# Second batch's scores in visits of six banks, a new order of q and k transposes, third batch's order, and the last output block in three pieces

## The chip, the cores and the metric

The kernel runs on one core of one Trainium2 chip. The metric is the device time of one execution in microseconds: the median of three runs before the change is 350.76 us (350.17 to 351.44). The engines are named as in the profile: PE is TensorE (matrix products; PEld its weight loads), DVE VectorE, ACT ScalarE, POOL GpSimd, SP the engine that issues transfers.

## The reference

An attention with beacon keys and values, and a mixer behind it. 8 batches, 8 heads, 576 queries, 16 beacons, head size 64.

```python
k_all = np.concatenate([beacon_k, k], axis=2)
v_all = np.concatenate([beacon_v, v], axis=2)
scores = scale * np.matmul(q, k_all.transpose(0, 1, 3, 2))
scores = np.where(causal, -1000000000.0, scores)
a = np.exp(scores - scores.max(-1, keepdims=True))
a /= a.sum(-1, keepdims=True) + 1e-09
x = np.matmul(a, v_all)              # then [batch, 576, 8 * 64]
...
h = x.transpose(0, 2, 1) @ U @ V     # U [576, 32], V [32, 576]
u = x + h.transpose(0, 2, 1)
out = u + np.maximum(u @ w_ch1, 0.0) @ w_ch2    # 512 -> 2048 -> 512
```

## The kernel before

**Tiling.** The work of attention is counted in pairs of heads: pair `p` is batch `p // 4` and heads `2 * (p % 4)` and the next, so pairs 0 to 3 are the first batch, 4 to 7 the second, 8 to 11 the third. The mixer's two large products run over eight full blocks of 512 rows and a last one (4608 rows are nine blocks). A block has 16 `g_unit`s (line 539: four products of 128x512 each, then a relu on ScalarE or VectorE into `gT`) and four output row blocks of 128, each in four quarters (`c_unit`, line 554: quarter `part` multiplies the slices `4 * part` to `4 * part + 3` of `gT` and `w2`, and the fourth adds u and stores).

**Steps of a pair.** `qkT_of(p)` has two units, which transpose q and k on TensorE into a bank of PSUM and copy them out on VectorE; their source is either the loaded tile itself or, after `regroup_of(p)`, a copy of it by token that VectorE makes. `scores_of(p)` gives units: the first two score groups, the last two, and the masks. There are four groups of keys; a group takes one bank for each head of the pair. A *visit* computes some groups, each into its banks, and ScalarE takes the exponential of each bank into the `expt` tiles. `visit` at line 373 takes any list of (pair, group), also of two pairs. Masks are applied by VectorE behind the exponentials; for pairs 0, 1 and 4 (`ON_PE`) instead by products of TensorE ahead of the scores. `av_of(p)` has a unit for each head: 15 products of probabilities and values into one bank, then VectorE's reciprocal and product into `xb`. The `expt` tiles are four, so pair p and pair p + 2 share them.

**PSUM.** `pst` (line 105) takes the bank that was given back longest ago in the order of the code, so an allocation waits for the user of eight allocations earlier.

**Order.** Every engine's order is that of the code (`manual_schedule`, line 788). The units of the mixer stand in `queue`, and `fill(n)` (line 754) issues the next n of them between steps of attention. When a batch's attention is done, `mix(b)` (line 771) puts the low-rank mixer's steps (`head`, `most`, `end`) and four empty places (`None`) into the queue and calls `feed`, which appends the blocks that have become possible. Block 0 covers the first 512 rows, all of the first batch; its 16 `g_unit`s and 16 quarters are the only units in the queue while the second batch's attention runs.

**Loads.** GpSimd issues the loads of q, k, v and of the weights, all in the order of the code: the first batch, then `emit_w1` quarters between loads of the second batch, then `emit_w2` (line 191) in two halves (slices 0 to 7 and 8 to 15), then the third batch (`load_batch(2)`).

**DMA transposes.** From batch 4 on q and k are transposed by DMA: `turns` (line 650) makes ten transfers, which SP issues (`kTs`, `qTs`; five blocks j each of k and q, in the order k0, q0, k1, q1, ...). SP also issues the transposes of `xb` into `uT`, those of `uT` into `ut`, and the stores.

**Last block.** `c_half` (line 581) computes the very last 128 rows in two halves of 256 columns, each stored by SP when it is done.

Of the kernel before, what the change touches and what calls it, by code (L numbers as in the profile page):

```python
# [18 lines left out]
P = 128  # L19
# [11 lines left out]
def kernel(  # L31
# [486 lines left out]
    def mlp_units(t0, n, dst, flip, turned=True, last=False):  # L518
# [59 lines left out]
                emptying(ps)  # L578
                nc.sync.dma_start(out=dst(i, m), in_=ob[:m, :])

        def c_half(i, part):
            hs = ds(DM // 2 * (part // 2), DM // 2)
            if part % 2 == 0:
                cps["t"] = pst([P, DM // 2], F32, name="cph")
            for dc in range(NDC // 2 * (part % 2), NDC // 2 * (part % 2 + 1)):
                nc.tensor.matmul(  # L586
                    cps["t"], gT["t"][:, dc, ts(i, P)], w2[:, dc, hs], start=(dc == 0), stop=(dc == NDC - 1)
                )
            if part % 2:
                ob = outp.tile([P, DM // 2], F32, name="oh", tag="ob")  # L590
                nc.vector.tensor_tensor(out=ob, in0=cps["t"], in1=gT["u"][:, i, hs], op=ALU.add)
                emptying(cps["t"])
                nc.sync.dma_start(out=dst(i, P)[:, hs], in_=ob)

        units += [lambda dc=dc: g_unit(dc) for dc in range(NDC)]
        for i in range((n + P - 1) // P):
            c = c_half if last and i == n // P - 1 else c_unit
            units += [lambda i=i, part=part, c=c: c(i, part) for part in range(4)]
        return units, g_part

# [49 lines left out]
    def turns(b):  # L650

        new_qT(b)
        kn, qn = Ls[b][1]
        us = []
        for j in range(NT):
            for n, dst, o, m in ((kn, kTs[b % 2], P * j, nk[j]), (qn, qTs[b], q0[j], nq[j])):
                us.append(
                    lambda n=n, dst=dst, o=o, m=m, j=j: nc.sync.dma_start_transpose(
                        out=dst[:, :, ds(o, m)], in_=n[:m, j, :, :].rearrange("p h d -> p (h d)")
                    )  # L660
                )
        return us

    HALVES = [slice(0, H // 2), slice(H // 2, H)]
    SETS = [slice(2 * c, 2 * c + 2) for c in range(NH2)]
# [67 lines left out]


    NF = 2
    ON_PE = (0, 1, 4)
    AHEAD = 16

    DT0 = 4
    LAG = 10  # L740
    HINT = 5

    FIRST = [3, 3, 2, 1]

    IDLE = [8, 1, 1, 0, 1]
    queue = []
# [7 lines left out]
    def fill(n):  # L754
        while n > 0 and queue:
            u = queue.pop(0)
            if u is not None:
                u()
            n -= 1

    def feed(b):

        while state["t"] < NBLK and 512 * (state["t"] + 1) <= S * (b + 1):
            t = state["t"]
            units, state["part"] = mlp_units(
                512 * t, 512, lambda i, m, t=t: rows[ds(512 * t + P * i, m), :], t % 2, t > 0, t == NBLK - 1
            )
            queue.extend(units)
            state["t"] += 1

    def mix(b):

        turned = b >= NF
        turn, head, parts = mix_units(xbs[b], S * b, turned)
        if turned:
            turn()
        n = 0 if not turned else LAG + 3 if b == B - 1 else min(LAG, len(queue) - 8)
        k = 2 if turned else 1
        most, end = parts
# [6 lines left out]
        feed(b)  # L786

    with tc.manual_schedule(engines={ENG.PE, ENG.Activation, ENG.DVE, ENG.SP, ENG.Pool}):
        load_first()
# [77 lines left out]
        begin(2, (3,))  # L867
        part(D2, 2)
        rest(2, 2, (act_copy, V), act_copy)
        t0, sc = qkT_of(4), scores_of(4)  # L870
        t0[1]()
        t0[0]()
        part(D3, 2)
        fill(4)
        fill(1)
        sc[0]()
        for u in qkT_of(5):
            u()
        fill(1)

        sc[1]()
        fill(1)
        sc = scores_of(5)
        sc[0]()

        NP1 = NF * NH2
        for p in range(NH2, NP1):
            b, c = divmod(p, NH2)
            if c == 0:
                load_batch(b + 1)  # L890
            seq = []
            masks = lambda: None
            if p + 2 < NP1:
                seq += [lambda i=i, p=p: qkT_of(p + 2)[i]() for i in range(2)]
            if p + 3 < NP1:
                seq.append(lambda p=p: regroup_of(p + 3))
            if p + 1 < NP1:
                seq.append(sc[1])
                masks = sc[2]
            av = av_of(p)  # L900
            if p + 2 == NP1:
                masks = lambda: None
                av = [lambda u=u, m=sc[3], i=i: (u(), m(i)) for i, u in enumerate(av)]
            seq += av
            sc = []
            if p + 2 < NP1:
                new_qT_of(p + 2)
                sc = scores_of(p + 2)
                seq.append(sc[0])
            seq.append(masks)  # L910
            done = 0
            for i, u in enumerate(seq):
                u()
                want = FIRST[c] * (i + 1) // len(seq)
                fill(want - done)
                done = want
            if c == NH2 - 1:
                mix(b)

        fill(AHEAD - 8)  # L920
        regroup_of(NP1)
        regroup_of(NP1 + 1)
        fill(8)
        t0, t1 = qkT_of(NP1), qkT_of(NP1 + 1)
        for u in t0 + [lambda: visit([(NP1, 0), (NP1, 1)])] + t1:
            u()
            fill(1)
        regroup_of(NP1 + 2)
        visit([(NP1, 2), (NP1, 3), (NP1 + 1, 0)])
        fill(1)  # L930
        tr = []


# [64 lines left out]
                    masks_of(p + 1)  # L998
                    fill(1)

        def slot(p, c, av, qk):

            if c == 0:
                regroup_of(p + 3)
                qk[0]()
                fill(1)
                masks_of(p)
                qk[1]()
                fill(1)
                go([(p + 1, 1), (p + 1, 2), (p + 1, 3)])  # L1010
                fill(1)
                av[0]()
                av[1]()
                fill(1)
            elif c == 1:
                regroup_of(p + 3)
                qk[0]()
                fill(1)
                masks_of(p)
                go([(p + 1, 0), (p + 1, 1), (p + 1, 2)])  # L1020
                fill(1)
                qk[1]()
                av[0]()
                fill(1)
                av[1]()
                fill(1)
            elif c == 2:
                regroup_of(p + 3)
                go([(p, 3), (p + 1, 0), (p + 1, 1)])
                fill(1)  # L1030
                masks_of(p)
                qk[0]()
                fill(1)
                av[0]()
                qk[1]()
                av[1]()
                fill(1)
            else:
                regroup_of(p + 3)
                go([(p, 2), (p, 3), (p + 1, 0)])  # L1040
                fill(1)
                qk[0]()
                fill(1)
                qk[1]()
                fill(1)
                masks_of(p)
                go([(p + 1, 1), (p + 1, 2), (p + 1, 3)])
                fill(1)
                av[0]()
                av[1]()  # L1050
                masks_of(p + 1)
                fill(1)

        for p in range(NP1, NP):
            b, c = divmod(p, NH2)
            if c == (1 if b >= DT0 else 0) and b + 1 < B:
                load_batch(b + 1)
            if c == (1 if b + 1 == DT0 else 2) and DT0 <= b + 2 < B:
                load_whole(b + 2)
            qk = qkT_of(p + 2) if p + 2 < min(NP, DT0 * NH2) else []  # L1060
# [10 lines left out]
            (slot if p < P6 else long_slot)(p, c, av_of(p), qk or [lambda: None] * 2)  # L1071
        mix(B - 1)
        guard()

# [106 lines left out]
```

## Time and profile before

| | |
|---|---|
| median of 3 runs | 350.76 us |
| profiled execution, own time | 351.05 us |
| its span | 349.4 us |
| granted TensorE clock, mean | 0.999 |
| TensorE on the chain that ended last | 94% |
| ScalarE, VectorE on it | 2%, 3% |
| DMA traffic | 41.89 MB, mean 120 GB/s |

The page shows busy time by engine, the span in 40 slices, the DMA queues, the chain of work that ended last, and the costliest groups of instructions. A row of the timeline has the start and the length in microseconds, the engine, the line of the code, the operation, what it writes and reads (`out<-in`), the shape, and how many instructions were merged; in brackets, the idle time of the engine before it and what the profile believes ended it. Matrix products are pipelined and their ends are modelled, so lengths of neighbours overlap; the difference of two starts is the better price. A row `DMA to landing us min/median/max` gives the time from the issue of a transfer to its last byte.

### The profile page before, as it was taken

How to read it: one execution, taken by the hardware profiler on the slowest of the kernel's cores; microseconds unless marked ns; L12 is line 12 of the kernel's file. 1: busy time of each engine (PE TensorE's matmuls, PEld its weight loads, DVE VectorE, ACT ScalarE, POOL GpSimd, SP SyncE). 2: the span in 40 equal slices, each digit the busy share in tenths (PEclk: the TensorE clock that was granted, in tenths of full speed). 3: DMA queues.
4: the chain of work that ended last, by engine and by line, in shares of the span. 5: the costliest groups of instructions: out<-in, count | busy, mean ns of one | idle time of the engine just before them, and what ended most of it. 6: DMA issues, size and time to landing. Idle time of an engine off the chain costs nothing.

```text
span 349.4 us, 7796 instructions
## 1 busy us (share of the span) xinstructions
PE 342.3 (98%) x3084; PEld 173.6 (50%) x3084; DVE 190.4 (55%) x492; ACT 163.7 (47%) x358; POOL 97.9 (28%) x137
## 2 busy tenths in 40 slices
PE   8999999999999999999999999999999999999995
PEld 4565565555554455444554545445444444444443
DVE  5776965788875653654465456535555642323311
ACT  5967851577823665167615753484334203302400
POOL 8886714553505447303740140000000000000000
PEclk9999999999999999999999999999999999999999
DMA  9999999999998999992999798713122314013011
GB/s 165 133 188 175 158 199 176 228 134 146 129 145 134 168 134 124 148 232 16 126 136 157 167 117 125 176 43 68 63 75 47 69 62 120 2 60 105 16 66 65
DMA packets 146636, 41.89 MB, mean 120 GB/s; under 512 B 131488, under 2 KB 142080, under 8 KB 146592
## 3 DMA queue, kind: packets, MB, share of 16 engines
q0 software_dynamic: 87440, 18.18, 69.8%
q1 hardware_dynamic: 58928, 22.84, 36.6%
q8 instruction: 26, 0.43, 0.6%
q10 hardware_dynamic: 224, 0.30, 0.3%
q14 instruction: 18, 0.15, 0.2%
HBM read 37.37 MB, written 9.44 MB: 134 GB/s over the span
## 4 chain that ended last, share of the span: by engine, by line
PE 94%; DVE 3%; ACT 2%; issue 0%
PE gps L534 36%; PE cps L560 35%; PE po L397 8%; PE sps L382 6%; ACT expt L354 2%; PE tps L275 1%; PE sps L348 1%; PE idle L250 1%; PE cph L586 1%; PE qtp L434 1%; PE tps L281 1%; PE ups L459 1%; DVE qT L308 1%; PE ups L413 1%; DVE xb L406 0%; DVE kT L308 0%
## 5 line engine op out<-in xcount | busy, mean ns | idle before, releaser
L534 PE MATMUL gps<-uT,w 128*128 128x512 f16 x576 | 136.2, 379 | 0.4 <-DVE qT L308 0.2
L560 PE MATMUL cps<-w,gT 128*128 128x512 f16 x560 | 130.8, 379 | 0.0
L388 ACT ACTIVATE expt<-sps 128x496 f16<-128x496 f32 x192 | 82.5, 534 | 71.7 <-PE sps L382 71.7
L547 ACT ACTIVATE gT<-gps 128x512 f16<-128x512 f32 x86 | 51.0, 620 | 79.2 <-PE gps L534 79.0
L534 PEld LDWEIGHTS <-w 128*128 128x128 f16 x576 | 51.8, 98 | 57.8 <-issue 2.5
L560 PEld LDWEIGHTS <-gT 128*128 128x128 f16 x560 | 50.8, 98 | 59.2 <-issue 6.2
L549 DVE TENSOR_SCALAR gT<-gps 128x512 f16<-128x512 f32 x58 | 39.9, 690 | 42.3 <-PE gps L534 40.9
L573 DVE TENSOR_TENSOR ob<-cps,ut 128x512 f32<-128x512 f32 x31 | 21.4, 691 | 48.3 <-PE cps L560 47.5
L218 POOL DMA_DIRECT2D vs<-in_v_dram x50 | 39.6, 806 | 17.4 <-PE gps L534 4.5
L397 PEld LDWEIGHTS <-expt 128*128 128x128 f16 (+1 forms) x960 | 36.3, 98 | 12.8 <-issue 1.0
L397 PE MATMUL po<-vs,expt 128*128 128x65 f16 (+1 forms) x960 | 38.9, 194 | 0.1
L406 DVE TENSOR_TENSOR xb<-po,rec 128x320 f16<-128x320 f32 x64 | 31.5, 492 | 2.2
L324 DVE TENSOR_TENSOR expt<-expt,bigmask 128x512 f16<-128x512 f16 x58 | 24.1, 416 | 6.7 <-ACT expt L388 6.7
L354 ACT ACTIVATE expt<-sps 128x496 f16<-128x496 f32 (+1 forms) x64 | 27.0, 606 | 1.0 <-PE sps L348 1.0
L405 DVE RECIPROCAL rec<-po 128x5 f32<-128x5 f32 x64 | 12.1, 188 | 26.9 <-PE po L397 26.7
L382 PE MATMUL sps<-qT,kT 64*128 64x80 f16 (+4 forms) x288 | 23.4, 281 | 0.4 <-DVE gT L549 0.3
L646 POOL DMA_DIRECT2D st<-in_q_dram x20 | 16.8, 856 | 11.3 <-DMA st<-in_k_dram 5.3
L382 PEld LDWEIGHTS <-kT 64*128 64x128 f16 x288 | 9.9, 94 | 18.8 <-issue 15.3
L200 POOL DMA_DIRECT2D vs<-in_beacon_v_dram x8 | 4.3, 536 | 53.5 <-PE po L397 53.5
L646 POOL DMA_DIRECT2D st<-in_k_dram x20 | 16.9, 867 | 4.3 <-DMA st<-in_q_dram 3.3
L446 DVE TENSOR_TENSOR uT<-ups,uT 128x496 f16<-128x496 f32 x24 | 14.5, 668 | 5.0 <-PE ups L459 5.0
L308 DVE COPY qT<-tps 128x576 f16<-128x576 f16 (+1 forms) x16 | 11.8, 735 | 3.9 <-PE tps L281 2.3
(97 smaller groups left out, 164.3 us busy)
## 6 DMA issues: line engine op xcount, KB each, us to landing
out_dram<-ob SPq DMA_DIRECT2D x35, 256.0 KB, 2.5
vs<-in_v_dram POOLq DMA_DIRECT2D x18, 128.0 KB, 7.2
w<-in_moe_w_ch_dram POOLq DMA_DIRECT2D x4, 512.0 KB, 6.8
w<-in_moe_w_ch_dram POOLq DMA_DIRECT2D x2, 1024.0 KB, 14.1
st<-in_k_dram POOLq DMA_DIRECT2D x12, 128.0 KB, 10.9
st<-in_q_dram POOLq DMA_DIRECT2D x12, 128.0 KB, 10.9
st<-in_k_dram POOLq DMA_DIRECT2D x2, 576.0 KB, 13.4
st<-in_q_dram POOLq DMA_DIRECT2D x2, 576.0 KB, 16.2
```

Source lines behind the costliest of these rows:

```text
L218: nc.gpsimd.dma_start(out=dst[a : a + nq[j], j, :, :], in_=src[hs, ds(q0[j], nq[j]), :].rearrange("h p d -> p h d"))
L324: nc.vector.tensor_tensor(out=e4, in0=e4, in1=bigmask, op=ALU.min)
L354: nc.scalar.activation(out=ex[i][:, ds(SLOT * g, gw[g])], in_=ps[g, i][:, 0 : gw[g]], func=AF.Exp, scale=scale)
L382: nc.tensor.matmul(ps[p, g, i][:, ds(o, w)], kT[hp, c, ds(P * ch, P)], qT[hp, c, ds(qa, w)], start=True, stop=True,)
L388: nc.scalar.activation(out=at[p][3][i][:, ds(SLOT * g, gw[g])], in_=ps[p, g, i][:, 0 : gw[g]], func=AF.Exp, scale=scale)
L397: nc.tensor.matmul(po[:, j, :], ex[0 : nk[c], ds(blk[(c, j)], P)], vs[0 : nk[c], ds(c * H * E + h * E, E)], start=(c == 0), stop=(c == j),)
L406: nc.vector.tensor_tensor(out=xb[:, :, ds(h * D, D)], in0=po[:, :, 0:D], in1=r.broadcast_to([P, NT, D]), op=ALU.mult)
L534: nc.tensor.matmul(g[:, 0:n], w1[:, cc, ts(dc, P)], uT[:, cc, ds(t0, n)], start=(cc == 0), stop=(cc == NCC - 1))
L547: nc.scalar.activation(out=gT["t"][:, dc, 0:n], in_=g[:, 0:n], func=AF.Relu)
L549: nc.vector.tensor_scalar_max(out=gT["t"][:, dc, 0:n], in0=g[:, 0:n], scalar1=0.0)
L560: nc.tensor.matmul(ps[:m, :], gT["t"][:, dc, ds(P * i, m)], w2[:, dc, :], start=(dc == 0), stop=turned and dc == NDC - 1, skip_group_check ...
L646: nc.gpsimd.dma_start(out=dst[a : m[j], j, :, :], in_=src[:, ds(q0[j], nq[j]), :].rearrange("h p d -> p h d"))
```

## The change

**Second batch.** The loop over pairs 4 to 7 with its counts (`FIRST`) is replaced by four lines of words, which a new function `play` issues. A word names a step and a pair: `f` one unit of the queue, `q` and `k` the two transposes, `r` the regrouping, `a` and `b` the values of the two heads, `m` (or `n`, `o` for one head) the masks, `e4:01` the groups 0 and 1 of pair 4 with masks by TensorE, and `v5:3,6:01` a visit of group 3 of pair 5 and groups 0 and 1 of pair 6. The old order, in the same words, from the first visit of pair 4 on:

```
f e4:01 q5 k5 f e4:23 f v5:01 q6 k6 r7 f v5:23 a4 b4 f v6:01 m5 f
q7 k7 v6:23 f a5 b5 f v7:01 m6 f
v7:23 a6 n7 f b6 o7 f
a7 b7 f
```

The new order is in the diff. From the first visit of pair 4 until `mix(1)` the queue gives 15 units instead of 11 (with the five ahead of it 20 instead of 16); behind `mix(1)` it gives 4 instead of 8 ahead of `regroup_of(8)`.

**Third batch.** The start of its order is written in words, and its four slots too. Against the old order, q11's transposes stand at the end of the first slot, ahead of the fill and of `regroup_of(12)`, where they stood behind it.

**DMA transposes.** `turns` issues k0, q0, q1, q2, q3, q4, k1, k2, k3, k4.

**Last block.** `c_piece` computes the last 128 rows in pieces of 256, 128 and 128 columns (48 products where there were 32); the last piece is stored by ScalarE.

```diff
-        def c_half(i, part):
-            hs = ds(DM // 2 * (part // 2), DM // 2)
...
+        def c_piece(i, part):
+            o, w, d0, d1 = [
+                (0, 2 * P, 0, NDC // 2), (0, 2 * P, NDC // 2, NDC), (2 * P, P, 0, NDC), (3 * P, P, 0, NDC)
+            ][part]
+            if d0 == 0:
+                cps["t"] = pst([P, w], F32, name="cph")
+            for dc in range(d0, d1):
+                nc.tensor.matmul(
+                    cps["t"], gT["t"][:, dc, ts(i, P)], w2[:, dc, ds(o, w)], start=(dc == 0), stop=(dc == NDC - 1)
+                )
+            if d1 == NDC:
+                ob = outp.tile([P, w], F32, name="oh", tag="ob")
+                nc.vector.tensor_tensor(out=ob, in0=cps["t"], in1=gT["u"][:, i, ds(o, w)], op=ALU.add)
+                emptying(cps["t"])
+                (nc.scalar if part == 3 else nc.sync).dma_start(out=dst(i, P)[:, ds(o, w)], in_=ob)
...
-        for j in range(NT):
-            for n, dst, o, m in ((kn, kTs[b % 2], P * j, nk[j]), (qn, qTs[b], q0[j], nq[j])):
...
+        k_of = lambda j: (kn, kTs[b % 2], P * j, nk[j], j)
+        q_of = lambda j: (qn, qTs[b], q0[j], nq[j], j)
...
+            for n, dst, o, m, j in [k_of(0), *map(q_of, range(NT)), *map(k_of, range(1, NT))]
...
+    def play(line):
+        for word in line.split():
+            what, p = word[0], int(word[1:].split(":")[0] or 0)
+            if what == "f":
+                fill(1)
+            elif what in "qk":
+                qkT_of(p)["qk".index(what)]()
...
+        for u in qkT_of(4)[::-1]:
+            u()
         part(D3, 2)
         fill(4)
...
+        for line in (
+            "f e4:01 q5 k5 f e4:23 f q6 v5:012 f a4 f",
+            "k6 f b4 r7 v5:3,6:01 f f m5 q7 k7 a5 b5",
+            "f v6:23,7:0 f m6 f a6 f v7:123",
+            "f b6 m7 f f a7 b7 f",
+        ):
+            play(line)
+            if line.startswith("f e4"):
+                load_batch(2)
+        mix(1)
+
+        fill(4)
         regroup_of(NP1)
         regroup_of(NP1 + 1)
         fill(8)
...
+        play("q8 f k8 f v8:01 f q9 f k9 f r10 v8:23,9:0 f")
...
+        third = (
+            "r11 q10 f m8 k10 f v9:123 f a8 b8 q11 f",
+            "r12 f m9 v10:012 f k11 a9 f b9 f",
+            "r13 v10:3,11:01 f m10 q12 f a10 k12 b10 f",
+            "r14 v11:23,12:0 f q13 f k13 f m11 v12:123 f a11 b11 m12 f",
+        )
```

More of the change, by code (lines that the diff above doesn't have):

```diff
@@ L786, in mix @@
         feed(b)
+    def play(line):
[5 more added lines that the diff above has]
+                qkT_of(p)["qk".index(what)]()
+            elif what == "r":
+                regroup_of(p)
+            elif what in "ab":
+                if what == "a":
+                    avs[p] = av_of(p)
+                avs[p]["ab".index(what)]()
+            elif what in "mno":
+                units = scores_of(p)
+                units[2]() if what == "m" else units[3]("no".index(what))
+            elif what == "e":
+                scores_of(p)[int(word[-1]) // 2]()
+            elif what == "v":
+                visit([(int(x[: x.index(":")]), int(g)) for x in word[1:].split(",") for g in x[x.index(":") + 1 :]])
     with tc.manual_schedule(engines={ENG.PE, ENG.Activation, ENG.DVE, ENG.SP, ENG.Pool}):
@@ L1059 @@
                 load_whole(b + 2)
-            qk = qkT_of(p + 2) if p + 2 < min(NP, DT0 * NH2) else []
+            qk = qkT_of(p + 2) if P6 <= p and p + 2 < min(NP, DT0 * NH2) else []
             if c == 0 and DT0 <= b + 1 < B and b != DT0:
@@ L1070 @@
                 fill_turns(tr, 2 * NT)
-            (slot if p < P6 else long_slot)(p, c, av_of(p), qk or [lambda: None] * 2)
+            if p < P6:
+                play(third[c])
+            else:
+                long_slot(p, c, av_of(p), qk or [lambda: None] * 2)
         mix(B - 1)
```

129 lines of the change are left out of this document (7 added, 122 removed).

## The prediction

> **What bounds the kernel now.** I read the page first (busy shares, then the chain that ended last), then TensorE's timeline, then the queues that feed it.
>
> ```profile
> span 349.4 us, 7796 instructions
> PE 342.3 (98%) x3084; PEld 173.6 (50%) x3084; DVE 190.4 (55%) x492; ACT 163.7 (47%) x358; POOL 97.9 (28%) x137
> ...
> DMA  9999999999998999992999798713122314013011
> ```
>
> TensorE is busy for 98% of the span, so a reordering can win only what lies between its products: changes of tile shape and short waits. The last line is the DMA engines' share in 40 slices of 8.7 us: full for the first half. Whatever is loaded there lands late, and a product moved earlier may meet a load that has not landed. So for every product that the change moves forward I look for its operands' landing.
>
> Of the changed stretch (second batch, from 33.48 us on) TensorE's timeline shows the end:
>
> ```profile
> 46.92 1.03 PE L534 MATMUL gps<-uT,w 128*128 128x512 f16 x4
> 47.78 1.08 PE L397 MATMUL po<-vs,expt 128*128 128x65 f16 x30
> 48.71 1.03 PE L534 MATMUL gps<-uT,w 128*128 128x512 f16 x4
> 49.66 0.62 PE L434 MATMUL qtp<-xb,Usb 112*32 112x128 f16 x20
> 50.21 1.04 PE L560 MATMUL cps<-w,gT 128*128 128x512 f16 x4
> ...
> 52.39 2.76 PE L560 MATMUL cps<-w,gT 128*128 128x512 f16 x12
> 54.99 0.39 PE L568 MATMUL cps<-ident,uT 128*128 128x128 f16 x4
> 55.21 0.31 PE L413 MATMUL uend<-ident,xb 80*128 80x80 f16 x4
> ```
>
> Durations overlap because products are pipelined; prices are differences of starts. A unit of four 512-wide products costs 0.86 us (46.92 to 47.78), 0.95 ahead of a tiled product (48.71 to 49.66); two heads of probabilities times values cost 0.93; four small identity products 0.22 (54.99 to 55.21).
>
> **The change part by part.** *Second batch, scores.* The six visits of four banks after 33.48 become four of six. The rows for both kinds:
>
> ```profile
> 33.48 0.58 PE L348 MATMUL sps<-qT,kT 64*128 64x496 f16 x4
> 33.99 0.71 PE L281 MATMUL tps<-ident,st 96*64 96x96 f16 x24
> ...
> 39.90 0.48 PE L348 MATMUL sps<-qT,kT 64*128 64x336 f16 x8
> 40.51 1.02 PE L534 MATMUL gps<-uT,w 128*128 128x512 f16 x4
> ...
> 44.72 0.48 PE L348 MATMUL sps<-qT,kT 64*128 64x336 f16 x8
> 45.13 0.63 PE L397 MATMUL po<-vs,expt 128*128 128x65 f16 x15
> ...
> 79.92 0.67 PE L382 MATMUL sps<-qT,kT 64*128 64x208 f16 x6
> 80.52 1.04 PE L534 MATMUL gps<-uT,w 128*128 128x512 f16 x4
> ...
> 91.90 0.79 PE L382 MATMUL sps<-qT,kT 64*128 64x496 f16 x10
> 92.62 0.47 PE L434 MATMUL qtp<-xb,Usb 112*32 112x128 f16 x20
> 93.02 1.04 PE L534 MATMUL gps<-uT,w 128*128 128x512 f16 x4
> ```
>
> Three pairs cost 3 x (0.51 + 0.41) = 2.76 us, plus a wait of 0.20 in the visit at 39.90 (0.61 against 0.41). In six-bank visits they cost 0.72 + 3 x 0.60 = 2.52, and one entry into the tiled shape (0.09) falls away. Together 0.53 us less.
>
> *Second batch, work between.* Up to the mix of the batch the old order fills with 16 units, the new one with 20: four `c_unit`s of the first block come out of the stretch behind the mix into this one. Their products cost the same in either place, if their weights are there. A `c_unit` quarter reads four slices of `w2`; slices 8 to 15 come with the second of the two `emit_w2` loads (line 195):
>
> ```profile
> L195 POOL DMA_DIRECT2D w<-in_moe_w_ch_dram x1: 921/921/921, 35.5 to 35.5; - x1
> DMA to landing us min/median/max: 12.0/12.0/12.0
> ...
> L195 POOL DMA_DIRECT2D w<-in_moe_w_ch_dram x2: 921/924/927, 35.5 to 36.4; - x2
> DMA to landing us min/median/max: 12.0/14.1/16.2
> ```
>
> The first is issued at 35.5 and takes 12.0, so it lands at 47.5. The second is issued at 36.4 and takes 16.2: it lands at 52.6. In the kernel before, slice 8 is due at 52.39 + 0.86 = 53.25, just behind it. In the changed kernel the third quarter, which begins with slice 8, stands ahead of the last pair's values (`f b6 m7 f f a7 b7 f`). When is it due? From 33.48 to 48.71 the old order runs eight gps units, all visits and eight heads of values (a4 to b7). The new one runs, ahead of slice 8, one gps unit more, two quarters, and two heads fewer (a7, b7): 48.71 + 0.87 + 1.73 - 0.93 - 0.53 = 49.85. So TensorE stands there until 52.6, some 2.7 us, and everything behind it (a7, b7, the last quarter, the mix) with it. The first quarter, due at about 47.6 with nothing late, meets slices landed at 47.5.
>
> What follows the landing sets the net: third quarter 0.87, a7 and b7 0.93, last quarter 0.87 + 0.22, then the mix's `qtp` of 0.40 (92.62 to 93.02) ends at 52.6 + 3.29 = 55.89. In the kernel before `qtp` ends at 50.21 with four quarters still owed, 4 x 0.86 + 0.22 = 3.66: 53.87. Net **+2.0 us**; the saving on visits is lost in the wait. Bounds: if the second load took 12.0 like the first, it would land at 48.4 and nothing would wait; the loads queued next took longer:
>
> ```profile
> st<-in_k_dram POOLq DMA_DIRECT2D x1, 576.0 KB, 17.8
> ```
>
> At 17.8 it lands at 54.2, +3.6. I take 16.2, this load's own row: GpSimd's loads keep their order and none of them waits for anything that the change moves.
>
> [...]
>
> Other engines are tight as well (the stretch, its length, then busy time of TensorE, its weight loads, VectorE, ScalarE, GpSimd, then the granted clock and the DMA share):
>
> ```profile
> 33.48:49.66 16.18, 16.05 (x229) 9.03 (x228) 14.30 (x40) 13.77 (x32) 9.02 (x12) 1.00 1.30 174
> ```
>
> VectorE works 14.30 of 16.18 us, ScalarE 13.77. Merged visits hand ScalarE six exponentials in one go, and VectorE's copies and masks queue behind each other; I expect up to 1 us of lateness around q7, k7, a5 and b5. That is covered by the wait for `w2`; without that wait it would cost up to 1 us.
>
> *Third batch.* Two places:
>
> ```profile
> 61.63 0.76 DVE L308 COPY kT<-tps 128x576 f16<-128x576 f16 x1 [0.38 <-PE tps L275]
> ...
> 75.25 0.75 DVE L308 COPY qT<-tps 128x576 f16<-128x576 f16 x1
> ...
> 76.06 1.02 PE L534 MATMUL gps<-uT,w 128*128 128x512 f16 x4 [0.23 <-DVE qT L308]
> ```
>
> Behind the mix the queue's empty places now fall between q8 and k8, so k8's copy (0.76 on VectorE) queues behind q8's of the same length, with one quarter of 0.86 + 0.22 and the transposes themselves to cover both before the next visit: 2 x 0.76 - 1.08 is 0.44 at the most, and part of such a wait is there already, so **+0.15** as an estimate. And q11's transposes move ahead of the copies of r12: the gps unit at 76.06 waits 0.23 for q11's copy to give back its bank. That copy now stands ahead of the copies of r12 on VectorE: **-0.25**. Bounds for both: 0 and twice the value.
>
> *Transposes.* In `turns` the q transposes go right behind the first of k. Batches four to seven take them; TensorE waits for them in one place:
>
> ```profile
> 177.38 1.24 SPq L658 DMA_TRANSPOSE kT<-st  x1
> ...
> L658 SPq DMA_TRANSPOSE qT<-st x1: 1916/1916/1916, 182.8 to 182.8; - x1
> ...
> DMA to landing us min/median/max: 8.4/8.4/8.4
> ...
> 190.77 0.48 PE L382 MATMUL sps<-qT,kT 64*128 64x336 f16 x8
> 191.59 0.38 PE L382 MATMUL sps<-qT,kT 64*128 64x496 f16 x2 [0.34 <-DVE gT L549]
> ```
>
> The product at 191.59 is pair 24's first group, which needs k0 and q0 to q3. q3, eighth of ten, is issued at 182.8 and lands 8.4 later at 191.2, so I read the wait as this DMA's, not as the VectorE instruction's that the row names. Its price: 0.82 from start to start, where the same products took 0.41 in the visit at 44.72 and left the tiled shape within that, so 0.45. As fifth, q3 goes out at 177.4 and lands near 186: **-0.45** (0 if the row's VectorE is right). The later k blocks then land last, in the places where the last q landed before, and pair 24's other groups are visited only a slot later.
>
> *The tail.*
>
> ```profile
> 341.76 0.69 DVE L573 TENSOR_TENSOR ob<-cps,ut 128x512 f32<-128x512 f32 x1 [2.76 <-PE cps L560]
> 345.25 0.42 DVE L591 TENSOR_TENSOR oh<-cph,ut 128x256 f32<-128x256 f32 x1 [1.32 <-PE cph L586]
> L593 SPq DMA_DIRECT2D out_dram<-oh x2: 332/332/333, 344.0 to 345.7; - x2
> DMA to landing us min/median/max: 2.3/2.4/2.6
> ```
>
> Products of 128 columns cost 0.055 (54.99 to 55.21 for four), half a 256-wide one, so TensorE ends as before. The last addition shrinks by half of 0.69 - 0.42: 0.13. The transfer's landing of 2.3 to 2.6 for 128 KB I leave: **-0.15**, between -0.5 and +0.3.
>
> [...] No row shows a store from ScalarE.
>
> Sum: +2.0 + 0.15 - 0.25 - 0.45 - 0.15 = +1.3 on the profiled execution's 351.05 (span 349.4 and 1.65 around it), which stands 0.3 above the median of 350.76: **352.1** for the median.
>
> **The rivals.** *The weights are there in time* (the other side). Place: slice 8 at 49.85; it decides from a landing below about 50. For it: the first half took only 12.0. Against: the 16.2 is of the very same load. Then the stretch gains 0.53 and 0.15 of `qtp`'s wait (0.55 against 0.40) and pays about 0.4 of VectorE's lateness; with the other parts about -1.0: 349.8.
>
> *The wait comes and the later gains don't* (q11's bank and q3's landing were not the causes, or the waits return elsewhere): +2.0 + 0.15 - 0.1: 352.8. For it: the row at 191.59 names VectorE.
>
> *A longer wait.* The load lands later than in this trace, at 54.2 in the bound: about 353.7. For it: the queue is full; against: nothing new is put in.
>
> **How the numbers follow.** Forecast 0.62 (own range 351.3 to 352.8), weights in time 0.17, later gains missing 0.14, longer wait 0.07. The range is 349.9 to 353.0: it takes in most of every case but the last. This kernel's measurement can tell about 0.3% from no change, 1.05 us. Slower than 351.81: 0.36 of the forecast, with 0.14 and 0.07: 0.57. Faster than 349.71: a little over half of the first rival, 0.10. The rest, 0.33, lies within.
>
> **What would show it.** In the changed kernel's profile: a gap of 2 to 3 us on TensorE around 50 to 52.6 ahead of an L560 product, ended by a `w` load, with `qtp` ending at about 55.9; VectorE and ScalarE idle there; no wait near 76 + 2 or 191 + 1.5; four score visits in the stretch. The prediction is wrong if TensorE runs through 50 to 53 without that gap, or if the landing has moved from 52.6 by more than 1 us.

## The result, and the profile after

| | before | after |
|---|---|---|
| median | 350.9 us (350.17 to 351.44, 8 runs) | 354.83 us (352.18 to 355.25, 8 runs) |
| ratio to before | | 1.0091, 95% interval 1.0061 to 1.012 |
| profiled execution, its own time | 351.05 us | 355.13 us |
| its span | 349.4 us | 353.4 us |
| mean granted clock in it | 0.999 | 0.995 |

The change makes the kernel 0.9% slower. The prediction had the sign (352.1 us), but the median lies outside its range of 349.9 to 353.0. The eight times fall into two groups: five of 354.78 to 355.25 us with a mean clock of 0.992 to 0.995, and three of 352.18 to 352.93 with 0.996 to 1.0. The profiled run is of the first. A second set of six runs of the same kernel, further down, has a median of 353.15 us with one run of the first kind.

The changed kernel's page: span, busy time, granted clock in 40 slices of 8.8 us.

```profile
span 353.4 us, 7828 instructions
PE 343.2 (97%) x3100; PEld 174.9 (49%) x3100; DVE 190.4 (54%) x493; ACT 163.7 (46%) x358; POOL 97.7 (28%) x137
...
PEclk9999998999999999999999999999999999999999
```

TensorE is busy 0.9 us longer with as much arithmetic, and one digit of the clock row, the seventh slice (53 to 62 us), is an 8. TensorE's timeline ahead of that place:

```profile
42.59 1.04 PE L534 MATMUL gps<-uT,w 128*128 128x512 f16 x4 [0.41 <-DMA w<-in_moe_w_ch_dram]
...
49.27 1.03 PE L560 MATMUL cps<-w,gT 128*128 128x512 f16 x4
52.73 1.69 PE L560 MATMUL cps<-w,gT 128*128 128x512 f16 x4 [2.42 <-DMA w<-in_moe_w_ch_dram]
54.21 1.86 PE L397 MATMUL po<-vs,expt 128*128 128x65 f16 x30
55.88 1.25 PE L560 MATMUL cps<-w,gT 128*128 128x512 f16 x4
56.97 0.39 PE L568 MATMUL cps<-ident,uT 128*128 128x128 f16 x4
57.28 0.47 PE L434 MATMUL qtp<-xb,Usb 112*32 112x128 f16 x20
57.68 1.04 PE L560 MATMUL cps<-w,gT 128*128 128x512 f16 x4
```

The first two quarters run at 47.94 and 49.27; the third waits 2.42 us for `w2`, as forecast. Ahead of them the gps unit at 42.59 waits 0.41 us for a load that the prediction did not look at: the last quarter of `w1` (`emit_w1`, line 189), which this order also needs earlier. It costs nothing here, since the wait for `w2` takes it in, and in no other profile with the new order do TensorE's products wait for it. Then, as was not forecast, the same products take longer: the third quarter 1.48 us from start to start in place of 0.86, the values a7 and b7 1.67 in place of 0.93. The windows over this stretch say why. (The columns: the window, its length, busy time and instructions of PE, PEld, DVE, ACT and POOL, then the granted clock, the DMA share and GB/s.)

```profile
51.00:52.00 1.00, 0.00 (x0) 0.00 (x0) 0.08 (x1) 0.00 (x0) 0.00 (x0) 1.00 1.33 214
52.00:53.00 1.00, 0.28 (x2) 0.15 (x2) 0.00 (x0) 0.00 (x0) 0.00 (x0) 0.97 1.31 197
53.00:54.00 1.00, 1.00 (x4) 0.39 (x3) 0.00 (x0) 0.00 (x0) 0.79 (x1) 0.50 1.32 201
...
55.00:56.00 1.00, 1.00 (x21) 1.00 (x19) 0.68 (x2) 0.00 (x0) 0.00 (x0) 0.50 1.32 204
56.00:57.00 1.00, 1.00 (x7) 0.36 (x5) 0.69 (x3) 0.00 (x0) 0.33 (x1) 0.83 1.97 167
```

VectorE and ScalarE stand idle too in the gap (0.08 and 0.00 of the microsecond from 51), so nothing that the profile shows but the load holds TensorE. Behind the gap the granted clock is 0.50. With 0.97 in the first of these windows and 0.83 in the last, that is 0.06 + 3 + 0.34 = 3.4 us at half speed: the 0.005 that the mean clock lacks (half of 3.4 in 353.4).

In the chain of waits the load stands by itself:

```profile
36.45 16.23 DMA w<-in_moe_w_ch_dram
52.68 0.04 issue
52.73 1.69 PE cps L560 x4
```

Issued at 36.45, landed at 52.68: 16.2 us, the number of the kernel before.

The three later places that the prediction priced: in TensorE's timeline the third batch, the start of its mix, and pair 24's first visit; then the lines of the tail's stores and of the closing steps (count, length in ns, first and last start):

```profile
80.97 0.42 PE L275 MATMUL tps<-ident,pr 96*128 96x96 f16 x6 [0.21 <-DVE gT L549]
...
96.75 0.47 PE L434 MATMUL qtp<-xb,Usb 112*32 112x128 f16 x20
...
194.90 0.69 PE L382 MATMUL sps<-qT,kT 64*128 64x336 f16 x10
195.52 0.82 PE L534 MATMUL gps<-uT,w 128*128 128x512 f16 x3
```

```profile
L596 SPq DMA_DIRECT2D out_dram<-oh x2: 332/332/332, 347.6 to 348.3; - x2
L596 ACTq DMA_DIRECT2D out_dram<-oh x1: 383/383/383, 349.2 to 349.2; - x1
DMA to landing us min/median/max: 1.7/2.2/2.8
...
L1070 DVEq EVENT_SEMAPHORE  x1: 21/21/21, 352.0 to 352.0; - x1
L1070 ACTq EVENT_SEMAPHORE  x1: 17/17/17, 352.3 to 352.3; - x1
```

The wait for q11's bank near 78 is gone, and one for k11's bank stands at 80.97 in its place (in this profile; the second one of this kernel, below, does not have it). The wait at 191 is gone: pair 24's first visit takes 0.62 from start to start. From the first product of the tail to the end of the span it is 8.2 us (345.17 to 353.4), where it was 7.8 (341.56 to 349.4).

### The profile page after: what moved, and what is told of

Read it like the earlier page. It is cut to its first block, busy times and chain, and to the rows that moved or that the text cites. A ratio compares the mean times of both kernels' runs of the same rounds, so it can differ in the third digit from the quotient of the medians.

```text
span 353.4 us, 7828 instructions
## 1 busy us (share of the span) xinstructions
PE 343.2 (97%) x3100; PEld 174.9 (49%) x3100; DVE 190.4 (54%) x493; ACT 163.7 (46%) x358; POOL 97.7 (28%) x137
## 4 chain that ended last, share of the span: by engine, by line
PE 83%; DMA 10%; DVE 3%; POOL 2%; issue 0%; SPq 0%; ACTq 0%; POOLq 0%
PE cps L560 34%; PE gps L534 31%; PE po L397 6%; PE sps L382 6%; DMA w<-in_moe_w_ch_dram 5%; DMA st<-in_q_dram 3%; DMA small<-in_moe_V_dram 1%; PE tps L275 1%; DMA stk<-in_k_dram 1%; PE cph L589 1%; POOL vs L218 1%; PE qtp L434 1%; PE ups L459 1%; DVE qT L308 1%; POOL st L203 1%; DVE pr L268 1%
## 5 line engine op out<-in xcount | busy, mean ns | idle before, releaser
L388 ACT ACTIVATE expt<-sps 128x496 f16<-128x496 f32 x216 | 92.7, 536 | 75.3 <-PE sps L382 74.7
L397 PEld LDWEIGHTS <-expt 128*128 128x128 f16 (+1 forms) x960 | 37.2, 99 | 13.4 <-issue 1.6
L397 PE MATMUL po<-vs,expt 128*128 128x65 f16 (+1 forms) x960 | 39.8, 195 | 0.1
L382 PE MATMUL sps<-qT,kT 64*128 64x496 f16 (+1 forms) x324 | 26.1, 281 | 0.2 <-DVE kT L313 0.2
L382 PEld LDWEIGHTS <-kT 64*128 64x128 f16 x324 | 11.1, 94 | 19.6 <-issue 15.7
L354 ACT ACTIVATE expt<-sps 128x496 f16<-128x496 f32 (+2 forms) x40 | 16.7, 641 | 0.7 <-PE sps L348 0.6
```

The source lines that it names most:

```text
L382: nc.tensor.matmul(ps[p, g, i][:, ds(o, w)], kT[hp, c, ds(P * ch, P)], qT[hp, c, ds(qa, w)], start=True, stop=True,)
L388: nc.scalar.activation(out=at[p][3][i][:, ds(SLOT * g, gw[g])], in_=ps[p, g, i][:, 0 : gw[g]], func=AF.Exp, scale=scale)
L397: nc.tensor.matmul(po[:, j, :], ex[0 : nk[c], ds(blk[(c, j)], P)], vs[0 : nk[c], ds(c * H * E + h * E, E)], start=(c == 0), stop=(c == j),)
```

## The experiments

The stretch that the change rewrites is compared by one length: from the end of the unit ahead of its first visit to the end of `qtp`. Before, with the four quarters that the new order has ahead of `qtp` (the prediction's 53.87), it is 53.87 - 33.48 = 20.39 us; after, 57.68 - 33.03 = 24.65. The other kernels' lengths come from the same two rows of their timelines. With sixteen fills the four quarters stand behind `qtp`, so its length is compared with 50.21 - 33.48 = 16.73 us.

| kernel | stretch, us | against before | gap ahead of the third quarter, us | median, us |
|---|---|---|---|---|
| after | 24.65 | +4.26 | 2.42 | 354.83 |
| after again | 22.00 | +1.61 | 1.72 | 353.15 |
| ten products in the gap | 23.20 | +2.81 | 0.31 | 354.02 |
| five products in the gap | 21.42 | +1.03 | none | 353.17 |
| `w2` in four loads | 20.45 | +0.06 | none | 351.67 |
| sixteen fills (against 16.73) | 18.93 | +2.20 | none | 353.12 |

The kernel before had medians of 350.54 to 350.95 in the three sessions of these runs.

**Products in the gap.** Ten products without use right ahead of the third quarter.

```diff
-            "f b6 m7 f f a7 b7 f",
+            "f b6 m7 f w10 f a7 b7 f",
```

> The changed kernel with ten products of 4 x 128 columns added (their result is not used) right behind the b6 visit, where TensorE otherwise stands still until the second half of w2 lands. Theory (the lost time behind the wait is the granted clock, which falls because TensorE stands idle for 2.4 us): the third quarter still starts when w2 lands, near 52.7, but the products behind it stay at 0.86 to 0.93 us and 216 ns each instead of 1.1 to 1.7 us, the granted clock is 1.0 in every run, and the time is 1.6 to 2.0 us lower than the profiled 355.1: about 353 us, in all runs alike. Rival (the products behind the wait are slow because they queue for something else, w2's DMA in SBUF or VectorE): they stay slow, and the time stays at 354 to 355 us.

TensorE's timeline of this kernel:

```profile
50.24 2.32 PE L250 MATMUL idle<-ident 128*128 128x512 f16 x10
52.88 1.02 PE L560 MATMUL cps<-w,gT 128*128 128x512 f16 x4 [0.31 <-DMA w<-in_moe_w_ch_dram]
53.73 1.08 PE L397 MATMUL po<-vs,expt 128*128 128x65 f16 x30
54.66 1.03 PE L560 MATMUL cps<-w,gT 128*128 128x512 f16 x4
```

The load lands no earlier, and the products behind it are at full speed: 0.85 and 0.93 us from start to start, the granted clock 1.00 in every window from 50 to 57 us. So the rival, that the slow products of the profile after queue for the load or for VectorE, does not hold. The profiled run took 353.26 us, 1.9 less than the one of after. But it is the fastest of the four, which lie between 353.26 and 354.47 us (median 354.02), not near 353 throughout; their mean clock is 0.996 to 1.0. As expected, the clock stays up where the gap is filled (1.00 behind 0.31 us, 0.50 behind 2.42 after); the time was forecast too low, and what makes the other three longer stays open. This median lies between the changed kernel's two, 354.83 and 353.15 us, and decides nothing by itself; the profile does.

**The changed kernel once more.** No edit.

> The changed kernel once more, with a second profile of it. Theory (two groups of runs: where w2's second half lands near 52.7, TensorE stands still for 2.4 us and its clock falls for 3.4 us; where the load lands a us or more earlier, the gap is shorter and the clock stays): runs near 355 us have a clock of 0.992 to 0.996, runs near 352.5 one of 0.997 to 1.0, and the profile of either kind shows gap and clock that go together. Rival (the clock falls by itself, without regard to the gap): a run with the full gap and full clock near 353.3, or a low clock with a short gap.

Median 353.15 us (352.19 to 355.41, 6 runs). This profile (350.6 us of span, 352.37 us) shows the other case; timeline, then a window:

```profile
51.77 1.02 PE L560 MATMUL cps<-w,gT 128*128 128x512 f16 x4 [1.72 <-DMA w<-in_moe_w_ch_dram]
52.63 1.09 PE L397 MATMUL po<-vs,expt 128*128 128x65 f16 x30
...
55.13 1.04 PE L560 MATMUL cps<-w,gT 128*128 128x512 f16 x4
```

```profile
53.00:54.00 1.00, 1.00 (x27) 0.76 (x23) 0.68 (x3) 0.00 (x0) 0.85 (x2) 1.00 1.30 200
```

The load landed 0.9 us earlier, the gap is 1.72 us, and the clock stays at 1.00. From the third quarter to the end of `qtp` it is 55.13 - 51.77 = 3.36 us (the prediction had 3.29), against 57.68 - 52.73 = 4.95 after: the clock cost 1.59 us. The other 1.06 us between the two stretches (24.65 and 22.00) are the third quarter's later start (52.73 against 51.77) and the stretch's earlier one (33.03 against 33.13). Of the 14 runs of the changed kernel, the six with a mean clock of 0.995 or less took 354.78 to 355.41 us; seven of the other eight took 352.18 to 353.81. The eighth, 354.88 us at a clock of 1.0, fits neither group, and what made it long stays open. Whether the faster runs without a profile had a shorter gap, or the same gap and no fall, is not shown.

**Five products in the gap.** As with ten.

> The changed kernel with five instead of ten added products (result not used) in the gap ahead of w2's second half, so that TensorE stands still for 1.2 to 1.4 us instead of 2.4. Theory (the clock falls only behind a gap of about 2.4 us): clock 1.0 behind the gap in every run, 352.5 to 353.5 us. Rival (any stop of more than 1 us brings the clock down): products of 410 to 430 ns behind the gap for 3.4 us, and 354.5 to 355 us.

Median 353.17 us (351.81 to 354.19, 6 runs), clock 0.997 to 1.0 throughout. In the profile the question did not come up (the 1.72 us of the run before speak against the rival, a fall behind any stop of more than 1 us); its lines on the issue of the `w2` loads, and its timeline:

```profile
L195 POOL DMA_DIRECT2D w<-in_moe_w_ch_dram x2: 887/910/933, 35.2 to 36.7; - x2
...
who waited for it (us, times):
busy tenths in 40 slices 0000200000000000000000000000000000000000
DMA to landing us min/median/max: 10.7/12.5/14.4
```

```profile
50.09 1.24 PE L250 MATMUL idle<-ident 128*128 128x512 f16 x5
51.17 1.03 PE L560 MATMUL cps<-w,gT 128*128 128x512 f16 x4
```

The same load took 14.4 us here and landed at 51.1, when the added products had just ended; nobody waited. So the landing itself moves by more than a microsecond from one execution to the next (52.7, 51.8 and 51.1 in these three profiles). Without the 1.08 us of the added products the stretch would be 0.05 us shorter than before: that is what the new order is worth in this execution, where the weights are there. It is the fastest of the six, and why the median lies 1.4 us above it is not shown.

**`w2` in four loads.**

```diff
-        for i in range(2):
-            dcs = ds(NDC // 2 * i, NDC // 2)
+        for i in range(4):
+            dcs = ds(NDC // 4 * i, NDC // 4)
```

> The changed kernel with the second weight matrix loaded in four transfers of four slices in place of two of eight, same queue and order. Theory (the unit due at 49.9 waits for one load of 1 MB that is complete only at 52.6): slices 8 to 11 land near 50 and slices 12 to 15 near 52.6, so the wait for the third quarter falls from 2.4 us to under 0.7 and a second one of up to 1 us comes ahead of the fourth quarter; no gap is long enough for the clock to fall: 350.5 to 352 us with the clock at 1.0. Rival (the whole queue is late, each transfer lands at the end of the burst): the wait stays at 2.4 us and the time at 354 to 355 us.

Median 351.67 us (350.67 to 353.0, 12 runs; ratio 1.0023, 1.0008 to 1.0038). Timeline:

```profile
49.72 1.89 PE L560 MATMUL cps<-w,gT 128*128 128x512 f16 x8
51.45 1.08 PE L397 MATMUL po<-vs,expt 128*128 128x65 f16 x30
52.53 1.02 PE L560 MATMUL cps<-w,gT 128*128 128x512 f16 x4
```

The second and third quarters run without a gap, and the fourth starts 0.15 us late. As the theory had it, most of the loss hung on the one load of 1 MB (16.2 us to its landing after; the four of half the size land 8.8 to 14.0 behind their issue): the median lies 0.7 us above that of the kernel before, where the two medians of the changed kernel lay 3.9 and 2.5 above. The new order still gains nothing over the old one (+0.06 for the stretch).

**Sixteen fills.** The new visits, but four `f` fewer in the lines and `fill(8)` behind the mix as before.

```diff
-            "f e4:01 q5 k5 f e4:23 f q6 v5:012 f a4 f",
-            "k6 f b4 r7 v5:3,6:01 f f m5 q7 k7 a5 b5",
-            "f v6:23,7:0 f m6 f a6 f v7:123",
-            "f b6 m7 f f a7 b7 f",
+            "f e4:01 q5 k5 f e4:23 f q6 v5:012 a4 f",
+            "k6 f b4 r7 v5:3,6:01 f m5 q7 k7 a5 b5",
+            "f v6:23,7:0 f m6 a6 f v7:123",
+            "f b6 m7 f a7 b7 f",
...
-        fill(4)
+        fill(8)
```

> The changed kernel with its new order of visits in the second batch, but four of its twenty fills moved behind the mix, so that sixteen units of the first batch's product stand ahead of the mix as before the change and no unit needs the second half of w2 before it has landed. Theory (six-bank visits cost TensorE nothing by themselves, the wait is made by the four units that moved ahead of the landing): no wait for w2, clock 1.0, 350.3 to 351 us. Rival (VectorE and ScalarE cannot follow the merged visits, so that waits for copies, exponentials and masks take the place of the wait for w2): no wait for w2, but 1 us or more of waits ended by VectorE or ScalarE between 33 and 50: 352 us or more.

The rival holds: median 353.12 us (352.87 to 354.1, 6 runs; ratio 1.0067, 1.005 to 1.0084) with no wait for `w2` and a clock of 1.0. The same work as in the kernel before, up to `qtp`, takes 18.38 us in place of 16.18. The window over it (columns as above), and who TensorE waited for in it:

```profile
33.77:52.15 18.38, 16.95 (x230) 9.15 (x230) 14.01 (x40) 13.80 (x32) 10.03 (x14) 1.00 1.27 173
```

```profile
PE tps L275 <- DVE pr L268: 0.6, 1, 0.6
PE po L397 <- DVE expt L324: 0.5, 2, 0.3
PE gps L534 <- DVE xb L406: 0.2, 1, 0.2
```

VectorE has no more to do (14.01 against 14.30), but it gets its work in lumps: pair 7's regrouped copies, masks and `xb` are late by turns. The view counts 1.3 us of gaps; the rest of the 2.2 lies in rows that count as busy (16.95 against 16.05), and what it is stays open. With twenty fills and the weights in time (`w2` in four loads) the same visits cost 0.06: the four units moved ahead of the mix were thus the cover of VectorE's lateness, and they are the same units that met the load.

**The old second batch.** The changed kernel with the loop of before for pairs 4 to 7.

> The changed kernel with the old loop for the second batch (four-bank visits, eight fills behind the mix); the third batch's order, the transposes' order and the tail in pieces stay. Theory (all the loss stands in the second batch: the wait for w2 and the clock behind it, near 3.7 us): no wait for w2, clock 1.0, and what is left is -0.5 from the transposes, +0.2 from the third batch and +0.4 from the tail: 350.8 to 351.3 us, the same as before. Rival (a good part of the loss comes from the later parts): 352 us or more.

Median 351.05 us (350.46 to 351.81, 11 runs; ratio 1.0005, 0.9995 to 1.0016): inside the theory's range. The loss stands in the second batch; what the change does elsewhere comes to 0.2 us, between -0.2 and +0.6 by the interval. The theory's sum has a part of luck: its -0.5 for the transposes is not a gain over the usual run, as the next two runs show.

**The transposes' order alone.** The kernel before with the new list in `turns`.

> The kernel before with one part of the change alone: in the later batches the DMA transposes of q go out right behind the first of k. Theory (TensorE waited 0.45 us at 191 for q3's transpose): that wait is gone and nothing takes its place, 350.4 to 350.5 us beside 350.95. Rival (the wait moves to the k blocks that now land last): 350.9 us, with a new wait of some tenths at a later slot.

Median 350.68 us (350.19 to 351.87, 12 runs; ratio 1.0006, 0.9994 to 1.0019). Its profile shows no wait at pair 24 and none in its place, yet the time does not fall. The next run says why.

**The kernel before once more.** No edit.

> The kernel before once more, for a second profile. Theory (its wait for q3's transpose at 191 is there in every run): a wait of 0.3 to 0.5 us ahead of pair 24's first group, and the wait for q11's bank near 76 as well. Rival (these waits belong to one execution): one or both are not there, which would say why the order of the transposes alone left the median where it was.

Median 350.53 us (350.23 to 352.08, 8 runs). Timeline of the second profile, at both places:

```profile
76.18 1.02 PE L534 MATMUL gps<-uT,w 128*128 128x512 f16 x4 [0.19 <-DVE qT L308]
...
190.90 0.76 PE L382 MATMUL sps<-qT,kT 64*128 64x336 f16 x10
191.59 1.69 PE L534 MATMUL gps<-uT,w 128*128 128x512 f16 x7
```

The wait for q11's bank is there again. Pair 24's first visit takes 0.69 us from start to start, 0.07 above the changed kernel's 0.62; in the first profile of before it took 1.13 (190.77 to 191.90, the next row there):

```profile
191.90 4.49 PE L534 MATMUL gps<-uT,w 128*128 128x512 f16 x20
```

The wait that I priced at 0.45 was there in one of the two profiles of this kernel, and the medians with and without the new order of the transposes (350.68 and 350.54 us in that session) do not show it.

**The tail, three ways.** All three are the kernel before with the transposes' order. Pieces, all stored by SyncE:

```diff
-                (nc.scalar if part == 3 else nc.sync).dma_start(out=dst(i, P)[:, ds(o, w)], in_=ob)
+                nc.sync.dma_start(out=dst(i, P)[:, ds(o, w)], in_=ob)
```

> The kernel before with the transposes' order, and with the tail in pieces of 256, 128 and 128 columns, but the last store issued by SyncE like the others. Theory (the 0.4 to 0.5 us that the new tail costs come from ScalarE's store): the time from the first product of the tail to the end falls back to 7.7 us or a little less, 350.3 to 350.5 us. Rival (the pieces themselves cost it, one store and one addition more in line): the tail stays at 8.1 us, and the time is 0.4 above that of the kernel with the transposes' order alone.

Halves, the second stored by ScalarE:

```diff
-                nc.sync.dma_start(out=dst(i, P)[:, hs], in_=ob)
+                (nc.scalar if part == 3 else nc.sync).dma_start(out=dst(i, P)[:, hs], in_=ob)
```

> The kernel before with the transposes' order, and with the old tail in halves of 256 columns, but the last store issued by ScalarE. Theory (ScalarE's store costs it): from the first product of the tail to the end 8.1 us in place of 7.7, and 0.4 us more than the kernel with the transposes' order alone: 350.9 us. Rival (the pieces cost it): 7.7 us, and 350.4 to 350.5 us.

Halves, the second stored by SyncE in two stores of 128 columns:

```diff
+                for o in (0, P) if part == 3 else ():
+                    nc.sync.dma_start(out=dst(i, P)[:, ds(DM // 2 + o, P)], in_=ob[:, ds(o, P)])
+                if part == 1:
-                nc.sync.dma_start(out=dst(i, P)[:, hs], in_=ob)
+                    nc.sync.dma_start(out=dst(i, P)[:, hs], in_=ob)
```

> The kernel before with the transposes' order and the old tail in halves of 256 columns, but the last half, computed and added in one piece, is stored by SyncE in two stores of 128 columns (64 KB, 512 bytes to a row). Theory (stores of 64 KB in rows of 512 bytes land later, 2.7 to 3.2 us after their issue in place of 2.3 to 2.6, and one more store in line adds its issue): 4.1 to 4.5 us from the end of the last addition to the end in place of 3.6 to 3.7, and 351.1 to 351.4 us. Rival (what costs is that the pieces' additions and stores follow each other at 0.9 us): 3.7 us, and 350.6 us.

| tail | first product to end, us | last landing to end, us | median, us |
|---|---|---|---|
| halves, SyncE (transposes' order alone) | 7.7 | 1.5 | 350.68 |
| pieces, ScalarE last (after, with the new second batch) | 8.2 | 1.9 | 354.83 |
| pieces, SyncE | 8.4 | 1.7 | 351.16 |
| halves, ScalarE last | 8.2 | 1.9 | 351.44 |
| halves, second in two stores | 7.7 | 1.4 | 350.71 |

The issues of the pieces stored by SyncE:

```profile
L596 SPq DMA_DIRECT2D out_dram<-oh x3: 332/333/1372, 343.4 to 345.1; - x3
```

The forecasts: for the pieces stored by SyncE and for the two small stores the rival holds, for the halves with ScalarE the theory, with 0.76 us in place of 0.4. So pieces and ScalarE's store each lengthen the tail by themselves. With SyncE, the third store's issue takes 1.37 us in place of 0.33, so its landing (2.6 behind the issue) gains nothing; why that issue takes so long stays open, since two stores issued back to back took 0.33 and 0.42. With ScalarE, the last store lands as fast as SyncE's (2.2), 0.1 us earlier than in the kernel before, counted from the tail's first product; but from the landing to the end it is 1.9 us in place of 1.4. Of the closing steps shown above, ScalarE's comes at 352.3, behind VectorE's at 352.0. That SyncE waits for its closing step, and that this makes the difference, is read from the order of these rows and not tested apart. Rows of 512 bytes cost nothing here: the two small stores land 1.8 to 2.0 behind their issue, the halves of the transposes' order alone 2.1 to 2.6. The median of the halves with ScalarE is 0.76 above that of the transposes' order alone, more than the tail's 0.5, and the profile of that kernel has a longer wait for q11's bank in the third batch (0.88 us in place of 0.30).

**Nineteen fills.** The changed kernel with `w2` in four loads, the old tail, and one unit back behind the mix:

```diff
-            "f b6 m7 f f a7 b7 f",
+            "f b6 m7 f a7 b7 f",
...
-        fill(4)
+        fill(5)
```

> The changed kernel with three repairs: w2 in four loads, nineteen in place of twenty fills ahead of the mix (the twentieth is made behind it), and the tail in halves stored by SyncE. Theory (the six-bank visits are worth no more than VectorE's lateness takes back, and the wait for w2, the clock and the tail were all the rest of the loss): no wait for w2, clock 1.0, 350.2 to 350.8 us, within 0.1% of the kernel before. Rival (with a fill less, VectorE's lateness comes out, as it did with sixteen): 351.5 us or more.

The rival holds: 351.97 us (351.25 to 352.79, 11 runs; ratio 1.0034, 1.0021 to 1.0046). TensorE's waits, up to the third batch's first visits:

```profile
PE sps L382 <- DVE kT L313: 0.9, 1, 0.9
PE cps L560 <- DMA w<-in_moe_w_ch_dram: 0.3, 1, 0.3
PE po L397 <- DVE expt L324: 0.3, 1, 0.3
```

One unit less, and a7 waits for pair 7's masks; and behind the mix, where the queue's empty places fall differently, k8's copy, priced at 0.15 in the prediction, costs 0.9; that the places are the reason is not tested. No version with the new second batch came out below the kernel before.

## Why the prediction was wrong

- **The gap ahead of the third quarter** came where and as it was forecast: 2.42 us (forecast 2.7), a load of 16.2 us, VectorE and ScalarE idle.
- **The step that failed** is "what follows the landing sets the net: third quarter 0.87, a7 and b7 0.93". These prices were taken at a granted clock of 1.00 (33.48 to 49.66 in the profile before), and the sum had no term for a clock that falls behind the gap. Behind the 2.4 us gap the granted clock was 0.50 for 3.4 us, and the 3.29 us of work took 4.95. With the clock kept up (after again) it took 3.36. This term of the net of +2.0 was short by 1.6 us, more than half of the 2.8 by which the profiled run (355.13) lies above its forecast (351.05 + 1.3); the tail (0.55 more than forecast) and the third batch (0.4 more) are most of the rest. Six of the eight runs in which the mean clock did not fall below 0.996 lie at 352.2 to 352.9 us, near the forecast 352.1; that nearness is partly luck: in the profile of after again the stretch cost 1.61 us in place of 2.0, because the load landed earlier, and the tail 0.5 (8.36 against 7.84) in place of -0.15. Which group the median falls in is partly chance: five of the first eight runs are in the slower one, one of the six later ones.
- **The landing** was taken from one execution: 16.2 us. It was 16.2 again in the profile after, but 15.6 and 14.4 in two others. TensorE was also 0.45 us ahead of its old times when it came to the stretch (33.03 against 33.48), which only lengthens a wait for a load that lands at the same time: no cost and no gain. From the stretch's start slice 8 was due 17.10 us later (50.13 - 33.03) and not 16.37 (49.85 - 33.48); 0.41 of the 0.73 is the wait for `w1`.
- **Six-bank visits, -0.53, and VectorE's lateness, up to 1 us, covered by the wait.** The cover was right: in the profile after no row up to the third quarter waits for VectorE or ScalarE. The price without cover was too low: with the sixteen fills of before the new order costs 2.2 us. Where the weights are in time and the four units cover (five products, `w2` in four), the new order gains nothing (-0.05, +0.06), not the 0.3 that the first rival gave it. That rival's own time, 349.8 us, also lay just outside the range from 349.9 that was to take in most of it.
- **Third batch, +0.15 - 0.25.** k8's copy costs 0.24, and q11's wait is gone, both as expected; k11's wait at 80.97 was not foreseen, and one profile of two has it. From the stretch to the next mix the profile after is 0.3 us longer (96.75 - 33.03 - 24.65 against 92.62 - 33.48 - 20.39), after again it is not.
- **Transposes, -0.45.** Seen as forecast between the first profile of before and the one of after (1.13 us to 0.62 for that visit), but it wasn't a gain over the kernel's usual run: the second profile of before has 0.07 of it.
- **Tail, -0.15, between -0.5 and +0.3.** +0.4, outside its bounds. The earlier landing came (0.1); what follows the landing was not in the sum.

The sum, by the profiled runs: stretch +4.26 (forecast 2.0), third batch +0.3 (-0.1), transposes -0.5 (-0.45), tail +0.4 (-0.15), the start -0.45 (not forecast): +4.0, the difference of the spans.

## What to carry to other kernels

A gap on TensorE may cost more than its length, as here (2.42 us, and another 1.59 behind it): price what stands behind a gap of such a length at both clocks, and give the slower one its chance (1.72 us left the clock up and 2.42 us did not, in one profile each). A wait read in one profile is the wait of one execution (pair 24's first visit took 1.13 us in one profile of the kernel before and 0.69 in the other); before a gain is booked on it, a second profile should show it again. And units that are moved ahead as filler can be the cover of another engine's lateness, as here (+0.06 us with them and the weights in time, +2.20 without): they have to be placed by what they themselves wait for, here a load of 1 MB that landed 16.2 us behind its issue.

## What the runs showed of the hardware

- Behind gaps of 0.31 us (ten products) and 1.72 us (after again) the granted clock stayed at 1.00; behind 2.42 us it fell to 0.50 for 3.4 us, from 52.93 to 56.35, that is 0.2 us after TensorE had gone on. One profile shows the fall, and the mean clocks of 0.992 to 0.995 in six of 14 runs speak for the same in those. They don't prove it by themselves, since the clock falls at the end of the program too (in the profile before at 348.54, 0.9 us ahead of the end): one run of the halves in two stores has a mean of 0.995 at 351.59 us.
- At the end, where TensorE has nothing more to do, windows of 0.1 us show when the clock falls to 0.50 behind its last product (whose end is modelled): after 2.1 us in the profile with ten products, between 2.3 and 3.5 in nine others, 4.4 in the profile after; in three the span ends 4.1 to 4.7 us behind that product and the clock is still at 1.00. The mean clocks of these profiles agree: 0.996 with ten products, 0.997 to 0.999 in the nine, 1.0 in the three. In twelve of the fourteen profiles, then, the clock was still up 2.4 us behind the last product. By these numbers the length of a gap alone does not decide, and one of 2.4 us may pass in one execution and not in the next. What else decides is not shown.
- One and the same load of 1 MB took 14.4 to 16.2 us from one profile to the next (five products 14.4, after again 15.6, ten products, halves in two stores and the second profile of before 16.0, before and after 16.2), while the DMA engines were 90% busy or more from 35.3 to 53.0 us, by the page of after.
- A store issued by ScalarE, which otherwise issues none near the end, landed 2.2 us behind its issue (halves with ScalarE; SyncE's, in the transposes' order alone, 2.1 to 2.6), but from the tail's first product to the end it was 8.2 us in place of 7.7.
